# A new order for a recurrent attention and feed-forward kernel: four more units turned by DMA, and the weights loaded through ScalarE

## The chip, the core and the metric

The kernel runs on one core of a Trainium2 chip. A core has five engines that run side by side and wait for each other through semaphores: TensorE (PE in the profile; its weight loads are PEld), VectorE (DVE), ScalarE (ACT), GpSimd (POOL) and SyncE (SP), which here only issues DMAs. TensorE writes to PSUM, eight banks of 512 floats in each of 128 partitions; the other data lie in SBUF, and inputs and outputs in HBM. The metric is the time of one execution on the device in microseconds (us). Before the change it was 156.16 us, the median of three runs (154.19, 156.16 and 156.34).

## What is computed

The first half is a recurrence over 768 steps, for 4 batches and 8 heads with a state of 48 by 48 each; the second half is a feed-forward block over all 3072 tokens.

```
for t in range(S):                                  # S = 768, D = 48
    cur     = (u * k_t)[:, None] * v_t[None, :]
    y_t     = r_t @ (state + cur)
    state   = w_t[:, None] * state + k_t[:, None] * v_t[None, :]
x    = y, heads side by side                        # 3072 x 384
h    = x @ w_in                                     # 3072 x 1024
solu = h * softmax(h)
ln   = (solu - mean) / sqrt(var + 1e-6) * g_ln
out  = ln @ w_out                                   # 3072 x 384, float32
```

## The kernel before, in words

The 768 steps are cut into 6 chunks of 128, and a **unit** is one chunk of one batch: 24 units, numbered chunk first, so that unit i needs the state that unit i-4 left. Each unit passes through the same steps. Four loads of 192 KB bring w, k, r and v (`LW`, `LK`, `LR`, `LV`), head by head in rows of 192 bytes. ScalarE takes the logarithm of w (`lw`), TensorE sums it along the chunk (`cum`), ScalarE exponentiates (`ex`), and VectorE multiplies k and r by the result (`kp`). The scaled k and r are turned, so that channels lie in partitions: either by eight TensorE transposes (`krk`, `krr`) and a copy out of PSUM (`kr`), or by one transposing DMA (`kt`). TensorE makes the scores (`M`), VectorE or ScalarE copies and masks them (`m`, with GpSimd's `sel` where ScalarE copies), and TensorE makes y from the scores, v and the state (`Y`; `y` copies it out). GpSimd makes the bonus term (`p`, `q`, sometimes `qh`, `dv`; VectorE's `dg` sums it). `S`, `et` and `st` make the next state, in units 0 to 19.

For the feed-forward half y is turned too, by three TensorE transposes and a copy (`X`, `xT`) or by one transposing DMA (`xt`). `H` multiplies by w_in, `e` exponentiates on ScalarE, `he` multiplies on VectorE, `hq` squares, `Oa` and `Ob` are the two halves of the product with w_out, and `sq`, `qm`, `lv`, `rs` and `o` normalise; `out` stores. There are two forms of this half. In the first, `H` is 24 products of 128 columns that give h already turned, and `Oa` and `Ob` also make the sums of e and of the squares by products of one column (fewer where GpSimd first adds e's halves, `ea`). In the second, for units that have an `ht`, `H` is 6 products of 512 columns, ScalarE sums while it exponentiates and squares (`sv` then prepares one scalar), one transposing DMA of 256 KB (`ht`) turns the product he, and `Oa` and `Ob` have no one-column products. Weights come in by `LI` (three loads of 512 KB) and `LO` (two of 768 KB), and `wi`, `gw`, `mn`, `mc` and `ce` cast, scale and centre them.

The order is written out by hand, as one long string, `ORDER`. A word such as `kr12.d` names a step, a unit and how it is done: for a copy the engine (a, d, p for ScalarE, VectorE, GpSimd), for a load its queue (nothing for SyncE, a for ScalarE, g for GpSimd), for a TensorE step its PSUM bank. The program goes through the words, and each engine gets its instructions in just this order: a wrapper, `InOrder`, ties every instruction to the one before it on the same engine. All of them are recorded in the wrapper, so nearly every line of the profile says L84 and groups are told apart by their tiles. DMA issues stand in the order of the engine that issues them, so a load on ScalarE's queue holds ScalarE's later work until it is issued. In the built program the DMAs of SyncE's and ScalarE's queues share eight completion semaphores in turn: each issue waits until the DMA eight places before it has landed.

```
        for hp in range(HP):                      # krk and krr: four TensorE transposes each
            pe.transpose(L["kr_ps"][:, j * HP + hp, :],
                         t[:, j, 2 * hp:2 * hp + 2, :].rearrange("t a d -> t (a d)"), ident)
...
    def turned_kr(i, x):                          # kt
        sp.dma_start_transpose(out=kr_s[i % NKP], in_=kp_t[i % NKP].rearrange("t a h d -> t (a h d)"))
```

Buffers are rings: 7 for each of the inputs, 10 for lw and v in bf16, 6 for the scaled and turned k and r, 4 for most of the feed-forward half. Before the change `kt` and `xt` serve units 16 to 23, and `ht` serves units 16 to 21.

Of the kernel before, what the change touches and what calls it, by code (L numbers as in the profile page):

```python
# [18 lines left out]


ORDER = """
LW0 ih0 LW1.a LW2.a LU0 LR0 LG0 LK0.a lw0 hot13.0 cum0.0 LR1 LK1.a LR2 LK2.a ex0 LV1 LW3 LV2.g LW4 LW5 ik0 lw2 kp0
us0.4 lw1 p0 cum1.5 LR3 LK3 uc0 ex1 cum2.0 kp1 ex2 LV3.g krk0.2 p1 kp2 q0 hot3.3 krk1.6 vb1.a LV0.a krr0 lw3 LR5
LK5 kr0.d krr1 LV4.g q1 hot1.0 M0.3 vb2.a kr1.d m0.d LK4.a LR4 krk2.7 p2 q2 lw4 lw5 dg0 krr2 M1.5 cum3.2 kr2.a LW6
ex3 S1.0 LW7 m1.d LV6.g hot1.1 cum5.6 LW9.a dg1 M2.4 kp3 vb0.a p3 dv0 ex5 LK7 vb3.a cum4.1 m2.d kp5 ex4 krk3.3 q3
et1 LR7.a dv1 LW8 LR6 LK6 S0.5 krr3 Y0.i7 et0 LV8.g dg2 kr3.a y0.a kp4 S2.6 et2 p4 st0 st2 lw6 LW10 vb4.a M3.1 lw7
dg3 krk4.3 Y1.i6 LR8.a p5 krk5.7 lw9 krr4 krr5 cum7.4 dv3 m3.d y1.a X1.6 ex7 q4 LV5.g kr5.a kr4.d dv2 LR9 LK8 LK9
xT1.a vb6.a st1 S3.1 M4.2 LI1.a X0.0 q5 kp7 et3 p6 cum6.4 xT0.d gs0.7 p7 ex6 Y2.i6 dg4 m4.d S4.0 gc0 vb8.a M5.2 LV7
lw8 kp6 Y3.i7 y2.a q6 LI2 krk7.4 st3 y3.a dv4 krk6.5 vb5.a cum8.6 et4 m5.d LI0.a S5.1 st4 ex8 dg5 cum9.2 LO1 ex9
krr6 krr7 LK10 kp8 q7 kp9 kr6.a krk8.0 et5 p8 krr8 wi1.p dg6 lw10 kr7.d X2.5 vb7.p LR10.a xT2.a kr8.a S6.6 Y4.i3  # L30
dg7 X3.5 xT3.d S8.7 et6 st5 y4.a dv5 LO0 S7.5 et8 et7 wi2.a LW14 st6 M6.3 Y5.i2 st8 M7.6 cum10.0 LW13 dv7 m6.d
wi0.p y5.a m7.d LR14.a ex10 X4.2 LV9.g st7 H0.3 xT4.d krk9.5 LV10 q8 LW12 qh8 LR11 gw7.a gw5.a dv6 LV13.g H1.6 LK12
LK14 kp10 e0 gw6.a Y6.n0 he0 krk10.1 krr9 X5.2 gw4.a gw2.d e1 gw0.a krr10 gw1.a gw3.p p10 y6.d xT5.d he1 kr9.d p9
dg8 kr10.a LW15 H3.3 e3 mn0.0 mc0 LR12 ce6.d Y7.i2 hq0.a H2.5 vb9.p y7.a lw14 ce4.d he3 ce0.p ce3.d ce2.d M10.1
LW11.a ce7.p ce5.p M9.3 S9.7 m10.a et9 m9.d ce1.p LK11 st9 LR15 cum14.0 e2 lw12 hq1.a he2 LV11.g Oa0.2 M8.3 Ob0
X7.7 ex14 m8.d LV12 kp14 q9 hq3.d lw11 xT7.a Oa1.5 LW16 LR13.a cum11.3 X6.7 Ob1 xT6.d LK13 sq0 LW17 cum12.0 krk14.7
ex11 dv8 q10 kp11 lw13 sq1 Y8.n6 krr14 qm1 qm0 ex12 H4.3 lv0 y8.d kp12 vb11.p lv1 ea3.p rs1 rs0 vb10.p ea2.p LR17
p12 o0.d sel10 krk11.6 o1.a cum13.0 kr14.d out1 dg9 hq2.a ex13 krr11 Oa3.2 kr11.d e4 out0 vb12.p q12 krk12.7 kp13
Ob3 lw15 sq3 lw17 LR16.a Oa2.5 cum15.0 krr12 qm3 he4 LK17.a p11 LK15 dv9 q11 krk13.6 Ob2 ex15 S10.3 S11.4 p14 lv3
LW21 kr12.d LV16.a rs3 kp15 LK16 LK19 sq2 et10 o3.a qm2 et11 Y9.i7 krr13 lv2 cum17.0 st10 lw16 y9.a rs2 st11 ex17  # L40
o2.a out3 ea4.p S12.2 kr13.d cum16.3 dg11 et12 H5.6 kp17 p15 ex16 st12 kp16 e5 hq4.a p13 dg10 X8.5 LW19 H7.0 vb13.p
e7 he5 H6.2 out2 e6 LV18.g dg12 he7 dv10 S13.4 LK18 Oa4.7 he6 et13 krk15.6 LR20 lw19 hq5.a Ob4 q13 M12.0 xT8.a sq4
krr15 LV15.g st13 dv12 m12.a qm4 qh13 Y10.n3 Oa5.2 M11.0 M13.4 Ob5 lv4 rs4 sel12 kr15.d LV17 o4.a q14 LV14 vb14.p
X9.7 m11.a hq6.d y10.d q15 X10.3 LW18 LR19 sq5 M14.0 m13.d ea6.p lw18 LK20 dv11 xT9.d qm5 LR22.a cum19.4 lv5 xT10.d
hq7.d rs5 H8.6 m14.d sel11 dg13 dv13 o5.a ex19 e8 LK22.a kp19 H9.2 out4 ea7.p Oa6.0 cum18.4 LW20 he8 e9 Ob6 LR18
S14.6 Y11.n7 lw20 ea9.p ex18 he9 sq6 p16 qm6 kp18 out5 lv6 H10.1 rs6 o6.d hq9.a et14 dg14 st14 e10 dv14 Y12.n4
Oa7.0 y11.d LW22 y12.d vb16.a cum20.5 hq8.a ex20 q16 Ob7 ea8.p LK21 sq7 kt16 vb15.a dg15 he10 kt17 lw22 kp20 qm7
p17 Y14.n3 Oa9.7 X11.4 xT11.a lv7 q17 out6 y14.d rs7 S16.2 Y13.n1 ea10.p y13.d et16 Ob9 o7.a M15.3 sq9 kt18 st16
qm9 m15.a M17.0 LW23 M18.5 Oa8.2 m17.d M16.3 lv9 cum22.0 rs9 o9.a vb17.a LK23 out7 p19 LV21 hq10.a ex22 out9 m18.d
Ob8 m16.d qh16 dg16 LV19 dg17 kt19 H11.5 sq8 lw21 Oa10.3 X12.4 p20 e11 qm8 kp22 xT12.a lv8 X13.7 xT13.d dv15 he11  # L50
dv17 sel15 q20 Ob10 rs8 sq10 q19 o8.a qm10 lv10 rs10 out8 X14.4 H12.0 Y17.n7 Y15.n2 xT14.d e12 dv16 hq11.a H13.5
e13 o10.d ea11.p y15.d he12 y17.d LR23 p18 out10 LV22 he13 vb18.p ea12.p hq12.a H14.3 Y16.n7 LR21 Oa11.0 q18
cum21.1 Ob11 e14 qh19 y16.d ex21 vb19.d he14 sq11 p22 hq13.a S15.6 qm11 kt22 lv11 rs11 dg18 dv18 o11.a Oa12.7 et15
X15.5 Ob12 ea13.p kt20 sq12 kp21 M19.3 xT15.d p23 qm12 xt16 lv12 st15 Y18.n2 H15.0 rs12 out11 ea14.p LV23 o12.a
dg20 m19.d lw23 e15 y18.d ea15.p dg19 he15 H16.6 dv19 out12 Y19.n5 cum23.2 Oa13.4 vb23.p hq14.a xt17 kt21 S17.0
ex23 kp23 q23 Ob13 p21 q22 LV20 xt18 vb21.a e16 sq13 Oa14.1 qm13 H17.2 kt23 lv13 y19.d et17 rs13 o13.a he16 sv16
vb20.p M21.4 hq15.a e17 M20.6 st17 out13 Ob14 sq14 dg23 m20.d Oa15.0 dv23 qm14 vb22.p m21.a S19.7 Ob15 xt19 he17
ht16 q21 lv14 rs14 o14.a sel21 sq15 qm15 lv15 et19 M23.3 m23.d out14 dv20 M22.1 ht17 rs15 H18.5 qh21 m22.a dg21
o15.a out15 e18 dv21 Y20.n4 y20.d dg22 xt20 hq16.a Y21.n2 S18.1 et18 y21.d dv22 hq17.a sel22 he18 H19.3 xt21 st18
Oa16.0 Oa17.2 e19 st19 ht18 hq18.a Y22.n1 Ob16 sq16 y22.d Ob17 he19 qm16 lv16 xt22 sq17 H21.5 sv18 Y23.n7 qm17  # L60
Oa18.4 sv17 rs16 lv17 rs17 e21 o16.d ht19 hq19.a o17.d H20.0 y23.d out16 e20 Ob18 sq18 out17 he21 xt23 H22.5 qm18
lv18 e22 hq21.a rs18 Oa19.7 ht21 H23.2 ea22.p sv19 o18.a Ob19 he20 he22 hq22.d sq19 qm19 Oa21.0 Oa22.4 e23 ht20
lv19 rs19 hq20.a Ob21 he23 sq21 ea23.p o19.a out18 Ob22 hq23.d qm21 out19 sv21 sq22 qm22 lv22 rs22 Oa20.3 o22.d
lv21 out22 rs21 o21.d Oa23.6 Ob20 sq20 qm20 sv20 lv20 Ob23 sq23 rs20 qm23 out21 lv23 rs23 o23.a o20.d out20 out23
"""

NIO, NLW, NKP, NWK, NHT = 7, 10, 6, 4, 4
# [559 lines left out]
```

## Time and profile before

| | |
|---|---|
| median of three runs | 156.16 us (154.19 to 156.34) |
| the profiled execution, its own time | 151.6 us |
| its span in the profile | 149.7 us |
| mean granted TensorE clock | 0.966 |
| busy: TensorE, VectorE, ScalarE, GpSimd | 130.6, 122.3, 122.1, 116.0 us |
| DMA | 31.50 MB, mean 210 GB/s |
| SyncE's queue (q1), ScalarE's (q10), GpSimd's (q0) | 74.1%, 14.3%, 4.4% of 16 engines |
| loads issued by SyncE, ScalarE, GpSimd | 71, 21, 11 |
| transposing DMAs, all by SyncE | 8 of k and r, 8 of y, 6 of he |

Busy is the time in which an engine has an instruction under way; TensorE's are pipelined, so that it can be busy and still not at its peak. The DMA share is the mean over the core's 16 DMA engines; as packets overlap it can pass 1. The profiled execution was 4.6 us shorter than the median of the timed runs.

### The profile page before, as it was taken

The numbers are of one execution on the slowest core, as the hardware profiler recorded it, in microseconds if no ns is written. First come the engines' busy times: TensorE is split into PE (matmuls) and PEld (weight loads), VectorE is DVE, ScalarE is ACT, GpSimd is POOL, SyncE is SP. The second block draws the span as 40 slices with busy tenths as digits, with TensorE's granted clock in tenths as the row PEclk, the third lists the DMA queues.
The fourth block names the chain that finished last, engine by engine and source line by source line (L and its number), as shares of the span: only waits on it lengthen the run. The fifth ranks groups of instructions, "written<-read, shape, count | busy, mean of one in ns | idle before, by whom it ended". The sixth has DMA issues, their size and how long they took to land. (4 is left out here: it accounts for less than half of the span.)

```text
span 149.7 us, 4668 instructions
## 1 busy us (share of the span) xinstructions
PE 130.6 (87%) x1804; PEld 95.3 (64%) x1809; DVE 122.3 (82%) x211; ACT 122.1 (82%) x266; POOL 116.0 (77%) x147
## 2 busy tenths in 40 slices
PE   6957439787599989999999999999999999899970
PEld 2325227565389856878977887689886566558540
DVE  5059759799588999999999989998997988776750
ACT  3297667696669988998998889998989999798951
POOL 7599587996799397999999999989999998103300
PEclk9999975899959999999999999999999999999999
DMA  5999999999999899989998999895978687479342
GB/s 104 255 287 262 278 239 210 246 286 316 362 322 254 174 204 226 204 215 246 244 239 180 224 220 217 174 203 146 198 184 185 119 194 210 100 173 166 88 158 105
DMA packets 112199, 31.50 MB, mean 210 GB/s; under 512 B 107161, under 2 KB 111266, under 8 KB 112178
## 3 DMA queue, kind: packets, MB, share of 16 engines
q1 hardware_dynamic: 91426, 24.26, 74.1%
q10 hardware_dynamic: 20048, 4.79, 14.3%
q0 software_dynamic: 704, 2.16, 4.4%
q8 instruction: 14, 0.23, 0.6%
q14 instruction: 7, 0.06, 0.1%
HBM read 22.03 MB, written 4.72 MB: 179 GB/s over the span
## 5 line engine op out<-in xcount | busy, mean ns | idle before, releaser
L84 PE MATMUL ps<-w,he 128*128 128x385 bf16 x192 | 42.4, 325 | 0.7 <-DVE st L84 0.4
L84 DVE TENSOR_TENSOR kp<-ps,kr_in 128x768 bf16<-128x768 f32 x24 | 22.9, 952 | 11.0 <-ACT ps L84 6.9
L84 POOL TENSOR_TENSOR p<-kr_in 128x384 bf16<-128x384 f32 x24 | 23.9, 1003 | 4.6 <-DMA kr_in<-in_k_dram 3.6
L84 PE MATMUL ps<-xT,win_sb 128*128 128x128 bf16 x432 | 27.0, 220 | 0.0
L84 POOL TENSOR_TENSOR ea<-e 128x512 bf16<-128x512 bf16 x15 | 17.7, 1184 | 11.0 <-ACT e L84 11.0
L84 PEld LDWEIGHTS <-win_sb 128*128 128x128 bf16 x432 | 25.2, 99 | 0.7
L84 ACT ACTIVATE e<-ps 128x1024 bf16<-128x1024 f32 x24 | 24.4, 1020 | 0.9 <-PE ps L84 0.8
L84 ACT ACTIVATE ps<-ps 128x768 f32<-128x768 f32 x24 | 19.1, 802 | 6.1 <-PE ps L84 6.0
L84 PE MATMUL ps<-one_col,hq 128*128 128x1 bf16 x144 | 23.6, 164 | 0.0
L84 DVE TENSOR_TENSOR he<-ps,e 128x1024 bf16<-128x1024 f32 x18 | 21.7, 1216 | 1.5 <-ACT e L84 1.4
L84 POOL TENSOR_TENSOR q<-p,u_bc 128x384 bf16<-128x384 bf16 x24 | 22.5, 939 | 0.2
L84 PEld LDWEIGHTS <-he 128*128 128x128 bf16 x192 | 18.0, 96 | 7.1 <-DMA he<-win_f 1.3
L84 DVE TENSOR_TENSOR m<-ps,keep 128x1024 bf16<-128x1024 f32 x18 | 21.7, 1216 | 0.4 <-PE ps L84 0.4
L84 POOL TENSOR_TENSOR dv<-vb,dg 128x384 bf16<-128x384 bf16 x24 | 19.9, 832 | 1.9 <-DVE dg L84 1.2
L84 PEld LDWEIGHTS <-kp 128*128 128x128 bf16 x208 | 13.9, 101 | 6.2 <-DVE kp L84 2.2
L84 ACT ACTIVATE lw<-w_in 128x384 bf16<-128x384 f32 x24 | 12.4, 525 | 4.2 <-DMA w_in<-in_w_dram 4.2
L84 PEld LDWEIGHTS <-kr 64*128 64x128 bf16 (+1 forms) x272 | 11.0, 97 | 6.2 <-issue 2.7
L84 PEld LDWEIGHTS <-hq 128*128 128x128 bf16 x144 | 11.2, 96 | 5.6
L84 ACT ACTIVATE hq<-he 128x1024 bf16<-128x1024 bf16 x13 | 13.7, 1053 | 0.0
L84 PE MATMUL ps<-ident,kp 128*128 128x128 bf16 x128 | 11.6, 231 | 1.6 <-DVE kp L84 1.6
L84 DVE TENSOR_REDUCE dg<-q 128x8 f32<-128x384 bf16 (+1 forms) x24 | 11.9, 500 | 0.4 <-POOL q L84 0.4
L84 PE MATMUL ps<-lw,uti_neg 128*128 128x384 bf16 x24 | 8.2, 344 | 3.2 <-DVE m L84 1.2
(97 smaller groups left out, 294.2 us busy)
## 6 DMA issues: line engine op xcount, KB each, us to landing
out_dram<-o SPq DMA_DIRECT2D x24, 192.0 KB, 2.3
w_in<-in_w_dram SPq DMA_DIRECT2D x20, 192.0 KB, 4.9
kr_in<-in_k_dram SPq DMA_DIRECT2D x18, 192.0 KB, 4.9
kr_in<-in_r_dram SPq DMA_DIRECT2D x17, 192.0 KB, 5.2
v_in<-in_v_dram POOLq DMA_DIRECT2D x11, 192.0 KB, 4.5
v_in<-in_v_dram SPq DMA_DIRECT2D x11, 192.0 KB, 4.3
wout_f<-in_moe_w_out_dram SPq DMA_DIRECT2D x2, 768.0 KB, 7.1
kr_in<-in_r_dram ACTq DMA_DIRECT2D x7, 192.0 KB, 5.1
```

Of the source, the lines that this page charges most:

```text
L84: made = make(*args, **kwargs)
```

## The change

Only the string `ORDER` changes; no function does. All its 43 lines are new, since the words stand in another sequence and most PSUM banks differ. What the words do is nearly the same, with these differences:

- Units 12 to 15 are turned by DMA. Their `krk`, `krr`, `kr`, `X` and `xT` go, and `kt`, `xt`, `ht` and `sv` come: `kt` and `xt` now serve units 12 to 23, `ht` units 12 to 21. With `ht` these four units take the second form of the feed-forward half.
- Queues: SyncE issues 63 loads instead of 71, ScalarE 33 instead of 21, GpSimd 7 instead of 11. All five loads of w_in and w_out are ScalarE's, and stand farther apart: they were between the 39th and the 42nd load of the order, and are between the 30th and the 49th.
- `ea` goes for units 2, 3 and 12 to 15, and comes for unit 5; `qh` serves nine units instead of five; `sel` five instead of six.
- Engines: VectorE has 2 `kr`, 2 `xT`, 1 `hq` and 1 `gw` fewer, 1 `m` and 1 `o` more; ScalarE has 2 `kr`, 2 `xT`, 1 `m`, 1 `o`, 5 `vb` and 1 `wi` fewer and 1 more `hq`; GpSimd has 5 more `vb`, 1 more `gw`, 1 more `wi`.
- Unit 2 leads the start instead of unit 0, and 16 products on zeros (`hot`) keep TensorE going instead of 18.

```
-LW0 ih0 LW1.a LW2.a LU0 LR0 LG0 LK0.a lw0 hot13.0 cum0.0 LR1 LK1.a LR2 LK2.a ex0 LV1 LW3 LV2.g LW4 LW5 ik0 lw2 kp0
+LW1.a LW0.a LW2 LR1.a lw2 hot10.0 cum2.0 lw1 LW5.a ex2 LV4.g LK2 LV6.g LR2 cum1.2 lw0 LK1 LW4.a ex1 hot2.4 cum0.4
...
-LW21 kr12.d LV16.a rs3 kp15 LK16 LK19 sq2 et10 o3.a qm2 et11 Y9.i7 krr13 lv2 cum17.0 st10 lw16 y9.a rs2 st11 ex17
+S10.1 dv8 S8.0 p11 LR16 H5.6 Y8.n2 ce2.d hq1.a et10 LV11 y7.a st13 M10.3 LK15 st10 m10.d kt12 LW19 p12 lw14 et8
...
-dv17 sel15 q20 Ob10 rs8 sq10 q19 o8.a qm10 lv10 rs10 out8 X14.4 H12.0 Y17.n7 Y15.n2 xT14.d e12 dv16 hq11.a H13.5
+p21 rs8 o8.d xt14 H12.4 dg17 lv11 rs11 p19 S17.1 dg16 ex23 out8 kp23 q19 e12 o11.a et17 dv16 dv17 H15.6 he12 M18.2
+Oa10.0 hq13.a Y16.n4 m18.d Ob10 p22 kt20 y16.d e15 sq10 p20 out11 st17 hq12.a q20 qm10 ht12 lv10 LV22.a qh20 he15
...
-lv18 e22 hq21.a rs18 Oa19.7 ht21 H23.2 ea22.p sv19 o18.a Ob19 he20 he22 hq22.d sq19 qm19 Oa21.0 Oa22.4 e23 ht20
-lv19 rs19 hq20.a Ob21 he23 sq21 ea23.p o19.a out18 Ob22 hq23.d qm21 out19 sv21 sq22 qm22 lv22 rs22 Oa20.3 o22.d
+e22 ea22.p o18.d o19.d out18 hq20.a sv20 Oa20.2 out19 he22 H23.3 sv21 out17 e23 Ob20 sq20 hq22.d ea23.p qm20 lv20
+rs20 he23 o20.a hq21.a Oa21.5 Oa22.0 Ob21 hq23.d Ob22 sq21 qm21 sq22 lv21 qm22 lv22 rs21 rs22 out20 o22.d o21.a
```

## The prediction, written before the changed kernel ran

> **What bounds the kernel now.** I read the page's busy times and its 40 slices first.
>
> ```profile
> span 149.7 us, 4668 instructions
> PE 130.6 (87%) x1804; PEld 95.3 (64%) x1809; DVE 122.3 (82%) x211; ACT 122.1 (82%) x266; POOL 116.0 (77%) x147
> ...
> PE   6957439787599989999999999999999999899970
> PEclk9999975899959999999999999999999999999999
> DMA  5999999999999899989998999895978687479342
> ```
>
> Every engine is busy for over three quarters of the span, so the sums settle little. In the slices (3.74 us each) TensorE has holes up to the eleventh slice, about 41 us, and hardly any from there to 140 us. DMA is full from the second slice on and thins out late. Next come the stretches, with each engine's busy time, and behind it the granted clock, the DMA share and GB/s.
>
> ```profile
> 0.00:62.00 62.00, 48.62 (x613) 33.82 (x615) 48.26 (x89) 45.09 (x85) 50.35 (x74) 0.92 1.08 252
> 62.00:86.00 24.00, 24.00 (x388) 19.72 (x386) 23.62 (x39) 22.16 (x47) 23.22 (x27) 1.00 0.99 220
> 86.00:120.00 34.00, 33.89 (x547) 26.10 (x546) 31.05 (x53) 32.00 (x68) 33.11 (x38) 1.00 0.88 183
> 120.00:141.00 21.00, 20.41 (x233) 13.50 (x233) 16.42 (x26) 19.11 (x51) 9.29 (x11) 1.00 0.77 151
> ```
>
> Up to 62 us the DMA share is over 1: the loads set the pace. From 62 to 120 us TensorE has no hole at all. What TensorE waited for from 40 to 136 us, in us, times and longest, bears that out:
>
> ```profile
> PE ps L84 <- DVE he L84: 0.6, 1, 0.6
> PE ps L84 <- DVE st L84: 0.4, 1, 0.4
> ```
>
> As a busy TensorE need not be at its peak, I took the spacing of its steps from its timeline (start, duration, what), where one starts right behind the other:
>
> ```profile
> 61.50 1.50 PE L84 MATMUL ps<-xT,win_sb 128*128 128x128 bf16 x24
> 62.83 0.39 PE L84 MATMUL ps<-ident,kp 128*128 128x128 bf16 x4
> 63.06 0.33 PE L84 MATMUL ps<-lw,uti_neg 128*128 128x384 bf16 x1
> ...
> 131.88 0.82 PE L84 MATMUL ps<-w,he 128*128 128x385 bf16 x4
> 132.54 1.46 PE L84 MATMUL ps<-win_sb,xT 128*128 128x512 bf16 x6
> 133.83 0.82 PE L84 MATMUL ps<-w,he 128*128 128x385 bf16 x4
> ```
>
> The reader sees H in its first form at 62.83 - 61.50 = 1.33 us, four transposes at 0.23, half an output in the second form at 0.66 and H in the second form at 1.29. Half an output in the first form took 0.81 (63.60 to 64.41, with `ea`) or 0.86 without. Adding such spacings over the order, 95.7 us of TensorE work stand at and behind the first H, which started at 43.55 us. That ends at 139.3 if nothing is late; TensorE really ended at 144.9. So **TensorE bounds the kernel from 43 us on** with 5.6 us lost, ahead of it the loads do, and the last 5 us are the chain of the last unit's normalisation and store.
>
> **The change, part by part.**
>
> *Units 12 to 15 on TensorE.* Their 64 step-wise transposes of k and r go: 8 groups of four, 1.8 us. `X` took 0.17 a unit: 0.7 us. H becomes 0.04 shorter a unit: 0.2 us. Eight halves of output go from 0.81 to 0.66: 1.2 us. `ea` gone for units 2 and 3 and new for 5 costs 0.1 net. Sum: **3.8 us less** in the stretch that TensorE bounds. The two `hot` products fewer lie ahead of it and count nothing; as they bridge a hole that the loads make, they would cost nothing either way.
>
> *The other engines.* VectorE: 2 `kr` (0.68), 2 `xT` (0.35), one `hq` (0.71), one `gw` (1.09) less, one `m` (1.22) and one `o` (0.61) more, four sums halved (0.20 each): 2.9 us less. ScalarE: 2 `kr` and one `m` (1.01), 2 `xT` (0.48), 5 `vb` (0.51), one `o` (0.58), one `wi` (1.04) less; one `hq` (1.05), eight read-outs of sums (0.20) and four `sv` (0.19) more: 4.8 us less. GpSimd: 5 `ea` (1.18), 4 load issues (0.94), one `sel` (1.14) less; 5 `vb` (0.52), 4 `qh` (0.55), one `gw` (1.27), one `wi` (1.04) more: 3.7 us less. None of them pays by itself, but each has to follow a TensorE that is 3.8 us quicker over 100 us. VectorE was busy for 23.62 of 24 us at 62 to 86, so there it has only its own saving to give.
>
> *Twelve more transposing DMAs.* SyncE issues all of them. Rows of SyncE's issues, with the shortest, median and longest duration in ns:
>
> ```profile
> L84 SPq DMA_TRANSPOSE kr<-kp x8: 1243/1262/2879, 86.5 to 118.1; - x8
> ...
> L84 SPq DMA_TRANSPOSE xT<-y x8: 1190/1210/2239, 109.3 to 133.6; - x8
> ...
> L84 SPq DMA_TRANSPOSE he<-win_f x6: 1240/1250/1278, 121.4 to 136.6; - x6
> ```
>
> Four of each: 4 x (1.26 + 1.21 + 1.25) = 14.9 us more on SyncE's queue, less 8 load issues at about 0.45 = 3.6 us. The landing comes 3.2, 2.4 and 3.1 us after the issue. Data: 4 x (256 + 96 + 256) KB = 2.49 MB. From 120 to 141 us, where only transposes and stores run, 21 us at 151 GB/s are 3.17 MB in 0.77 x 21 = 16.2 us of DMA time, 5.1 us a MB; so 12.7 us of DMA time are added, all of it where loads still come. Room up to the 1.08 of the start: 24 x 0.09 + 34 x 0.20 = 9.0 us. This is close. Bounds: nothing, if transposes and loads overlap (from 106 to 108 us the trace has both at once at a share of 1.45), and 12.7 - 9.0 = 3.7 us late. I take nothing, since from the middle of the kernel on most loads lay ready long before use: for v of unit 18 the landing was at 77.6 and its use at 105.9.
> [...]
>
> *ScalarE's 33 load issues instead of 21.* An issue waits for the landing of the DMA eight places earlier, and holds ScalarE. The timelines of ScalarE and TensorE show what that costs when it goes wrong:
>
> ```profile
> 38.20 0.41 ACTq L84 DMA_DIRECT2D kr_in<-in_r_dram  x1
> 38.65 0.48 ACT L84 COPY xT<-ps 128x384 bf16<-128x384 bf16 x1 [2.34 <-DMA v_in<-in_v_dram]
> ```
>
> ```profile
> 39.18 0.33 PE L84 MATMUL ps<-ident,y 128*128 128x128 bf16 x3 [1.99 <-ACT xT L84]
> ```
>
> ScalarE stood 2.34 us before a load of r could be issued, the copy of `xT` behind it was late, and TensorE stood 1.99 us for that copy. Two of 21 issues did so (the other 1.26 us); most hide behind the running instruction. At that rate 12 more cost ScalarE 2.1 us; bounds 0 and 12 x 2.34. I take no net change, since ScalarE saves 4.8 us.
> [...]
>
> *The start and the spread weights.* Up to 62 us at 252 GB/s 15.6 MB came: 3.15 MB of weights, in some 9.5 us at the 316 to 362 GB/s of the slices they came in, and 63 loads, (62 - 9.5) / 63 = 0.83 us each. The second H stands behind 50 loads and all weights, with 94.1 us of TensorE work at and behind it: 41.5 + 9.5 + 94.1 = 145.1. In the new order the worst such place is the third H, behind 57 loads, with 86.2: 47.3 + 9.5 + 86.2 = 143.0, so 2.1 us less and not 3.8. Where the loads hold the start, 1.7 us of the gain go. Bounds 0 and 1.7; I take 0.9.
>
> *The end.* The last `ht20` landed 5.2 us after its issue instead of 3.1, and the output behind it started only then. The new order puts `Oa20` ahead of the last H, with more outputs behind: bounds 0 and -2.1, taken -0.4.
>
> Sum: -3.8 + 0.9 - 0.4 = **-3.3 us**. On the profiled execution's own 151.6 us (149.7 span and 1.9 around it) that is 148.3, or -2.2%. The median stood 3.0% above that execution; 148.3 x 156.16 / 151.6 = **152.8 us**. A measurement of this kernel tells about 2% from no change: 153.0 and 159.3 are the borders.
>
> **The rivals.** (1) *The gain is not followed.* VectorE, ScalarE or one of ScalarE's late issues holds TensorE, which gives its 3.8 us back as new holes. For it: 23.62 of 24 us on VectorE. Against: 31.05 of 34 later on. Time: 0 to -1.5 us, middle 155.4; chance 0.22. (2) *The transposes take over, and the kernel is slower.* The place is SyncE's queue and the DMAs behind it between 62 and 120 us. For it: room 9.0 against 12.7 us, and at 106 to 138 us SyncE already issued nearly back to back. Decided at 9.0 us of DMA time for the twelve, 0.75 us each; beyond that loads and turned tiles are late and TensorE waits, its gain gone: +3.7 us, 155.3 x 1.030 = 160.0. Against: landing was long ahead of use. Chance 0.28. (3) *The saving is not there*, as the transposes moved were hidden: excluded by a TensorE without holes while they ran, so I fold it into (1).
>
> **How the numbers follow.** The forecast has 0.50, spread from 149.0 (start free, `ht20` on time, first scaled k about 1 us earlier: -6.9 us) to 154; 0.41 of it is under 153.0. Rival 1 adds 0.02 to faster and 0.20 to same; rival 2 has 0.24 beyond 159.3 and 0.04 below. Faster 0.43, same 0.33, slower 0.24. The range goes from 149.0 to 160.5.
>
> **What would show it.** TensorE's records 162 fewer; no hole over 0.6 us between 45 and 135 us; its end near 141.5. A DMA share above 0.95 from 62 to 120 us without new waits on landings would clear the transposes. Wrong would be: TensorE waiting for `kr`, `xT` or `he` landings, or ScalarE idle ahead of load issues for more than 5 us in all.

## The result

| | before | after |
|---|---|---|
| median of the timed runs, same chip | 155.18 us | 168.12 us (166.37 to 169.23, 4 runs) |
| ratio to before, 95% interval | | 1.094 (1.069 to 1.119): slower |
| the profiled execution: its own time, its span | 151.6, 149.7 us | 166.37, 164.5 us |
| TensorE's last product ends | 144.9 us | 159.6 us |

The forecast was 152.8 us, the range 149.0 to 160.5; the kernel came out beyond the range, even beyond the slower rival's 160.0. The ratios here and below use only runs within 1.5% of the fastest of the same kernel, so they are not the quotients of the medians. First the page of the kernel after: its header, then TensorE's busy time, the granted clock and the DMA share in 40 slices of 4.11 us.

```profile
span 164.5 us, 4367 instructions
PE 134.2 (82%) x1640; PEld 94.2 (57%) x1647; DVE 123.0 (75%) x207; ACT 115.9 (70%) x267; POOL 111.8 (68%) x148
...
PE   6726747895647999999999979299999899799970
PEclk9985765579995589999999999959999999999996
DMA  5999999999999999946899999996799577775613
```

TensorE has 164 records fewer (162 were forecast, and the two programs have 1808 and 1646 products), and yet is busy 3.6 us longer. Its row is no longer full from the twelfth slice on: there is a hole near 103 us and several late ones. The clock row, all but full in the kernel before, has fives and sixes in the first 60 us and a five at 107 us. The same stretches as in the prediction (each engine's busy time, then granted clock, DMA share, GB/s):

```profile
0.00:62.00 62.00, 43.79 (x467) 30.68 (x469) 39.10 (x74) 34.47 (x66) 45.31 (x69) 0.75 1.11 251
62.00:86.00 24.00, 23.62 (x381) 18.53 (x380) 23.66 (x39) 22.64 (x49) 20.27 (x26) 1.00 0.86 176
86.00:120.00 34.00, 29.54 (x405) 22.26 (x406) 26.91 (x44) 24.78 (x57) 25.79 (x30) 0.95 1.05 212
120.00:141.00 21.00, 20.23 (x238) 12.32 (x238) 20.12 (x32) 17.48 (x50) 16.24 (x22) 1.00 0.82 171
```

Up to 62 us TensorE did 467 products where it had done 613, at a mean clock of 0.75 instead of 0.92, and from 86 to 120 us it stood 4.5 of 34 us. What TensorE waited for from 40 to 136 us, and the longest of ScalarE's waits over the whole run (us, times, longest):

```profile
PE ps L84 <- DVE he L84: 3.5, 2, 3.2
PE ps L84 <- ACT m L84: 2.2, 2, 1.2
PE ps L84 <- DVE kp L84: 1.9, 3, 0.9
```

```profile
ACT ps L84 <- DMA kr_in<-in_k_dram: 5.5, 2, 4.4
...
ACT lw L84 <- POOL q L84: 4.0, 1, 4.0
ACT e L84 <- DMA w_in<-in_w_dram: 3.5, 1, 3.5
...
ACT vb L84 <- DMA kr_in<-in_r_dram: 2.2, 1, 2.2
```

TensorE hardly waited for a landing; it waited for what VectorE and ScalarE make. But ScalarE's own list is full of landings of tiles that the named instruction does not read: `ps` is no reader of k, `vb` none of r. In each case a load issue stands between the two and was the one that waited. ScalarE's waits that end with a landing sum to 20.7 us after, 7.8 us before; without those of the logarithm `lw` for w, which it does read, to 18.8 and 3.6 us.

To place the loss I took two sums from the traces, behind 43 us, where TensorE sets the pace: TensorE's idle time, and half of its busy time in the stretches at half clock (the clock's records are 1.0 or 0.5 and nothing else).

| kernel | TensorE's end | idle behind 43 us | at half clock behind 43 us | work in it | so lost |
|---|---|---|---|---|---|
| before | 144.9 | 1.8 | 1.2 | 1.2 | 0.6 |
| after | 159.6 | 10.8 | 13.6 | 12.5 | 6.2 |

Idle 9.0 us more and half clock 5.6 us more make 14.6 of the 14.7 us by which TensorE ended later. That is a little too good: at 45 us the work still to come, added at the prediction's spacings, ended at 136.0 against 139.1 us, so the kernel after was 3.1 us ahead then, and about 3 us more were lost in ways that these two sums don't show. (These projected ends are estimates: with the mean spacings of the two traces instead, the lead at 45 us comes out as 1.4 us.) At 65 us the same sum ended at 148.2 against 142.3, at 110 us at 155.9 against 144.3: the loss came in steps, at 45 to 65 and at 95 to 110 us.

### The profile page after: what moved, and what is told of

Its sections match the earlier page's. It is cut to its first block, busy times and chain, and to the rows that moved or that the text cites. A ratio compares the mean times of both kernels' runs of the same rounds, so it can differ in the third digit from the quotient of the medians.

```text
span 164.5 us, 4367 instructions
## 1 busy us (share of the span) xinstructions
PE 134.2 (82%) x1640; PEld 94.2 (57%) x1647; DVE 123.0 (75%) x207; ACT 115.9 (70%) x267; POOL 111.8 (68%) x148
## 4 chain that ended last, share of the span: by engine, by line
PE 28%; DMA 24%; POOL 15%; ACT 12%; issue 9%; DVE 5%; SPq 4%; ACTq 2%; DVEq 0%; POOLq 0%
PE ps L84 28%; DMA w_in<-in_w_dram 8%; DMA kr_in<-in_k_dram 5%; POOL q L84 5%; POOL p L84 4%; DMA kr_in<-in_r_dram 3%; SPq L84 3%; ACT e L84 3%; DMA win_f<-in_moe_w_in_dram 3%; DMA he<-win_f 3%; ACT hq L84 2%; DMA xT<-y 2%; ACT o L84 2%; POOL vb L84 2%; ACTq L84 2%
## 5 line engine op out<-in xcount | busy, mean ns | idle before, releaser
L84 DVE TENSOR_TENSOR kp<-ps,kr_in 128x768 bf16<-128x768 f32 x24 | 22.7, 952 | 14.7 <-ACT ps L84 14.7
L84 PE MATMUL ps<-xT,win_sb 128*128 128x128 bf16 x336 | 24.0, 237 | 0.4 <-DVE kp L84 0.2
L84 PEld LDWEIGHTS <-win_sb 128*128 128x128 bf16 x336 | 22.5, 108 | 1.9 <-issue 0.6
L84 DVE TENSOR_TENSOR m<-ps,keep 128x1024 bf16<-128x1024 f32 x19 | 23.1, 1216 | 0.3 <-PE ps L84 0.2
L84 DVE TENSOR_TENSOR he<-ps,e 128x1024 bf16<-128x1024 f32 x14 | 17.0, 1217 | 6.9 <-ACT e L84 6.9
L84 POOL TENSOR_TENSOR ea<-e 128x512 bf16<-128x512 bf16 x10 | 11.5, 1154 | 14.9 <-ACT e L84 13.8
L84 PE MATMUL ps<-one_col,hq 128*128 128x1 bf16 x112 | 18.4, 164 | 0.4 <-DVE hq L84 0.4
L84 PE MATMUL ps<-kr 64*128 64x128 bf16 x192 | 10.5, 237 | 5.7 <-DVE kr L84 3.0
L84 PE MATMUL ps<-win_sb,xT 128*128 128x512 bf16 x54 | 14.1, 379 | 0.3
L84 DVE TENSOR_TENSOR st<-ps,et 128x384 bf16<-128x384 f32 x20 | 10.6, 548 | 3.5 <-ACT et L84 3.5
L84 DVE TENSOR_TENSOR win_f<-ps,e 128x1024 bf16<-128x1024 f32 x10 | 12.2, 1216 | 0.5 <-ACT e L84 0.4
```

The costliest lines, as they stand in the source:

```text
L84: made = make(*args, **kwargs)
```

## The experiments

The times are medians; the ratio is to the kernel before, timed on the same chip at the same time.

| edit | us | ratio (95%) |
|---|---|---|
| the order of after, the queues of before | 165.83 | 1.081 (1.066 to 1.096) |
| the order of before, the queues of after | 168.99 (163.81 to 170.26) | none on record; before: 153.73 |
| start of before, rest of after | 166.16 | 1.104 (1.096 to 1.112) |
| start of after, rest of before | 168.10 | 1.115 (1.105 to 1.125) |
| after, units 12 to 15 turned by TensorE | 168.01 | 1.102 (1.087 to 1.117) |
| after, 29 load issues from ScalarE to SyncE | 172.81 | 1.148 (1.136 to 1.160) |
| before, three load issues from SyncE to ScalarE | 170.05 | 1.129 (1.121 to 1.138) |
| after, three load issues off ScalarE | 162.05 | 1.058 (1.049 to 1.068) |
| after, five load issues off ScalarE | 161.15 | 1.063 (1.054 to 1.072) |
| after, 33 idle products in TensorE's holes | 164.48 | 1.077 (1.069 to 1.084) |
| before, 17 idle products in TensorE's holes | 154.66 | 1.011 (0.994 to 1.028) |
| before, units 12 to 15 turned by transfers | 171.78 | 1.129 (1.118 to 1.139) |
| the same, transfers placed by the trace | 164.51 | 1.077 (1.068 to 1.086) |
| the same, eleven stores by GpSimd | 164.16 | 1.080 (1.067 to 1.092) |
| after, eleven stores by GpSimd | 169.44 | 1.117 (1.108 to 1.126) |
| after, all three remedies | 163.08 | 1.073 (1.062 to 1.083) |
| before, twelve transposing transfers more | 167.41 | 1.091 (1.077 to 1.105) |
| before, twelve plain copies more | 162.79 | 1.060 (1.042 to 1.077) |

### Which part of the change: queues, order or turned units

Two kernels exchange the queue letters of the loads (51 words each), one turns units 12 to 15 back, one puts nearly all load issues on SyncE, and two join the halves of the orders at about 60 us.

```
 e1: LW1.a LW0.a LW2 LR1.a ...   ->  LW1.a LW0 LW2.a LR1 ...      (order of after)
 e4: kt12 ... xt12 ... ht12 sv12 ->  krk12.7 krr12 kr12.d ... X12 xT12 ...  (units 12 to 15)
 e6: LW4.a LK5.a LR5.a ...       ->  LW4 LK5 LR5 ...              (29 words)
 s1: words of before up to its second H, then what is left, in the order of after
```

The order of after with the queues of before:

> The changed kernel, with every load on the queue that it has in the kernel before; the order of the words stays. Theory A (ScalarE stands at its load issues until the DMA eight places back has landed; waits of ScalarE that end with a landing grew from 7.8 to 20.7 us): ScalarE's waits on landings fall to 8 to 11 us and the span from 164.5 to 150 to 156. Theory B (the twelve new transposing DMAs fill the DMA): no change, 162 to 166. Theory C (the sequence itself is poor, whatever the queues): 160 to 166, with the holes of TensorE up to 60 us still there.

The order of before with the queues of after:

> The kernel before, with every load on the queue that the changed kernel gives it. Theory A: ScalarE's waits on landings rise from 7.8 to 15 us or more and the span from 149.7 to 156 to 162. Theory B and theory C: within 2 us of 149.7.

After, units 12 to 15 turned by TensorE:

> The changed kernel, with units 12 to 15 turned by TensorE again and their feed-forward half in the first form (without the added halves of e); queues and the rest of the order stay. Theory A and theory C: it stays slow, 162 to 170. Theory B: the span falls to 150 to 156.

After, without ScalarE's issues:

> After, with all load issues of ScalarE behind the first few moved to SyncE's queue at the same places of the order, so that ScalarE never stands at a load issue that waits for an earlier landing (20.7 us in after, 7.8 us in before). If ScalarE's standing is the cause: the difference of 12.9 us comes back, 155 to 158 us. If not: some 20 more issues on SyncE (about 0.45 us each, 9 us) and the same waits now standing in SyncE's queue, ahead of the transposing transfers: 165 to 172 us, with TensorE waiting for landings instead of for ScalarE.

The two joined orders:

> The order of before up to its second H (about the first 60 us), and the order of after for everything that is then left. By the projected end (time plus TensorE work still to come) after had lost 5.6 us on before by 60 us and another 12.5 us behind that. Theory 'start' (the loads of the first 60 us come late, and the rest of after only carries that on, because its loads and turned tiles then meet at 82 to 98 us): with before's start the later loss goes too, 150 to 156 us. Theory 'rest' (the order behind is itself what loses): 12.5 us of it stay, 162 to 166 us. Theory 'fit' (each half is fitted to the other's times, so any mixture loses at the seam): over 165 us.

> The mirror: the order of after up to its H of unit 1 (about the first 62 us), then the order of before for what is left, so that units 12 to 15 are turned by TensorE. Theory 'start': the late loads of the start do it, 162 to 168 us, and the curve of the projected end goes on rising behind 62 us as in after. Theory 'rest': only the 5.6 us of the start are lost, 157 to 160 us, with a flat projected end behind 65 us. Theory 'fit': over 165 us with new holes right behind the seam.

Measured: medians between 165.8 and 172.8 us. Turning the four units back changed nothing (168.01 against 168.12), so in the kernel after the turned units, taken whole, are not what costs: they seem to give back just the 3.8 us that they should save. Giving the queues back brought 1%, which lies inside the intervals; giving the order back ranged from 163.81 to 170.26 us and brought nothing clear of noise. Yet with the queues of before ScalarE's waits that end with a landing fell from 20.7 us to this one:

```profile
ACT lw L83 <- DMA w_in<-in_w_dram: 4.0, 1, 4.0
```

That meets the condition of theory A, but not its time of 150 to 156 us, so ScalarE's held issues alone are not the loss. In that profile TensorE waited for turned tiles instead, 5.0 us behind 43 us where it had been 1.1. The joined orders were as slow as after in both directions; of the three theories written down only "fit" allows both, the first of them by 1 us. The kernel with all but four of ScalarE's issues taken away was the slowest of the six: SyncE then had those issues and their waits ahead of the transposing transfers, and TensorE's waits for turned k and r rose to 5.6 us. What follows is that no part of the change, taken out by itself, gives the loss back: every mixture was some 8 to 15% slower than the kernel before. That the order of before is fitted to its own queues is a reading of this, not shown by it. So I went to single instructions.

### Three load issues on ScalarE

The kernel before, with three words changed (of the five weight transfers two were ScalarE's already, so three move; the expectation's twelve is wrong):

```
-... LI2 ... LO1 ... LO0 ...
+... LI2.a ... LO1.a ... LO0.a ...
```

> Before, with only the twelve transfers of the two weight matrices issued by ScalarE as in after, all else untouched. With all of after's queues in the order of before it was 169.0 us, its delay coming in one jump of 11 us at 34 to 41 us. If the weights on ScalarE make that jump (each of their issues waits for the landing eight places back and holds the casts and read-outs behind it): 162 to 169 us, with 15 to 20 us of ScalarE's waits ending with a landing. If the other moved queues (k, r, v, gates) make it: 154 to 158 us.

Measured: 170.05 us, 17 us for three letters. The timelines of ScalarE and TensorE in that kernel (start, duration, what; in brackets the idle time before it and what ended it) show how:

```profile
46.73 0.48 ACT L84 CAST y<-ps 128x384 bf16<-128x384 f32 x1
54.92 0.37 ACTq L84 DMA_DIRECT2D kr_in<-in_r_dram  x1
55.42 0.80 ACT L84 ACTIVATE ps<-ps 128x768 f32<-128x768 f32 x1 [8.21 <-POOL vb L84]
```

```profile
57.25 0.48 PE L84 MATMUL ps<-st,kr 128*128 128x96 bf16 x4 [6.41 <-DVE kp L84]
```

ScalarE reached the load of r of unit 14 at 47.2 us and could issue it at 54.92; `ex` of unit 10 stood behind it for 8.2 us, and TensorE 6.4 us for that, of the 18.4 us by which it ended later. In the kernel before the same load was issued at 42.24 without a wait. Nobody had touched it. The built program tells why. The transfers of SyncE and ScalarE share eight completion counters in turn, and an issue waits until the counter's previous transfer has landed: in the trace of after, 26 of ScalarE's 33 issues have that landing on record, none went ahead of it, and 16 went 0.02 to 0.08 us behind it. The turns go by the order of the instructions in the built program, which is not that of the list: with more loads on ScalarE, its issues come farther back there. In the kernel before, r of unit 14 takes its turn behind three SyncE loads that stand later in the list, and follows k of unit 10, which had landed at 42.11 us; with three letters changed it takes it behind thirteen such loads and follows k of unit 11, which landed at 54.8 us. Summed over ScalarE's issues that have a transfer eight turns ahead, such overtaking transfers of SyncE are 32 in before (21 issues in all), 78 here, and 204 in after (33 issues).

In the kernel after this is the chain of waits from 40 to 66 us (start, duration, what):

```profile
39.91 5.69 DMA kr_in<-in_r_dram
45.60 0.02 issue
45.62 4.62 DMA win_f<-in_moe_w_in_dram
...
53.28 5.85 DMA w_in<-in_w_dram
59.13 0.02 issue
59.15 0.37 ACTq L84
...
59.62 0.04 ACT e L84
```

The third part of the first weight matrix could only be issued 0.02 us after r of unit 12 had landed, whose counter it takes; and at 59.15 us v of unit 14 could only be issued when w of unit 17 had landed. Behind that issue stood the first exponential `e` of the hidden layer, for 3.5 us, for a v that is used at 75 us. So I took these issues away:

```
-... LI2.a ... LO1.a ... LV14.a ...
+... LI2 ... LO1 ... LV14.g ...
```

> After with three load issues taken from ScalarE's queue: the third part of the first weight matrix and the second half of the other one to SyncE, v of unit 14 to GpSimd. In after ScalarE stood 2.2, 2.5 and 3.5 us at these three before the casts, copies and read-outs behind them, and the chain of waits from 40 to 66 us runs through the first and the third. Issue theory: of these 8.2 us about 5 come back in the first output of the hidden layer (it starts at 59.6 us in after), and with it some of the half clock, 161 to 164 us. If the first 60 us are bound by the loads themselves or the later part loses on its own: 166 to 169 us.

Measured: 162.05 us, ratio 1.058 against 1.094. Three of 921 words are worth 6.1 us of the medians. TensorE ended at 155.1 us, 4.5 us earlier: idle 10.0 us, half clock 6.8 us. At 85 us the projected end was 143.7 us, level with the kernel before; the rest was lost behind that. The chain there led to the next such issue, in the kernel after at 99 to 103 us:

```profile
102.12 0.89 POOL q L84
103.01 0.36 ACTq L84
...
104.16 0.70 ACT e L84
104.86 0.02 issue
104.89 1.24 DVE he L84
```

That is v of unit 23, used at 136 us. The chain names GpSimd's `q`, which ended at the same time, but the issue needs nothing of it. It needs the buffer, free since GpSimd had cast v of unit 16:

```profile
95.03 0.50 POOL L84 CAST vb<-v_in 128x384 bf16<-128x384 f32 x1 [1.00 <-DMA v_in<-in_v_dram]
```

And it needs its completion counter, whose transfer eight turns earlier is r of unit 22: that landed at 102.92 us, and the issue went at 102.99. So the counter held this issue too, and not the buffer, as the next expectation has it. ScalarE stood 4.0 us there with the exponential of unit 11 behind, and TensorE had its hole of 3.2 us. Two words more:

```
-... LR21.a ... LV23.a ...
+... LR21 ... LV23.g ...
```

> The kernel with three issues moved (162.05 us), and two more taken from ScalarE: v of unit 23 to GpSimd, whose own cast frees that buffer (in after ScalarE stood 4.0 us at this issue, at 99 to 103 us, for a load that is used at 136 us, and the exponential of unit 11 stood behind it; in the kernel with three issues moved 3.4 us), and r of unit 21 to SyncE (1.2 us). Issue theory: TensorE's hole of 2.2 us at 99.5 us goes and with it the half clock at 103.0 to 106.4 us that takes 1.7 us, 158 to 159.5 us. If the loads of 82 to 98 us are late in any case (v of units 16 and 19 land 0.1 to 0.8 us ahead of their use): 161 to 163 us, with a hole of the same length elsewhere.

Measured: 161.15 us, ratio 1.063 (1.054 to 1.072), so no change against 1.058. The wait and the hole of 2.2 us went, as the theory of issues has it, and TensorE's idle time behind 43 us fell from 10.0 to 8.6 us; but it ended only 0.5 us earlier. Holes of 1.2 and 0.6 us at 90 to 93 us (for turned k and for scaled k) are in the kernel with three issues moved as well, 1.9 us earlier, so this execution was already behind there, and the half clock came at 93.6 to 97.0 us instead of 103.0 to 106.4. The time is that of the second expectation; its reason, that the loads of 82 to 98 us are late in any case, is not shown by it, as no new hole of the same length opened.

### The half clock

The kernel after in windows of 4 us from 44 us (TensorE's busy time first, then weight loads, VectorE, ScalarE, GpSimd; granted clock, DMA share, GB/s), and TensorE's timeline:

```profile
44.00:48.00 4.00, 2.52 (x52) 2.12 (x50) 1.44 (x3) 1.98 (x6) 3.60 (x4) 1.00 1.07 220
48.00:52.00 4.00, 2.76 (x31) 1.93 (x32) 3.53 (x5) 1.51 (x3) 1.71 (x2) 0.62 1.07 267
52.00:56.00 4.00, 3.28 (x23) 1.94 (x23) 2.53 (x3) 4.00 (x7) 3.53 (x5) 0.50 0.97 262
56.00:60.00 4.00, 4.00 (x47) 4.00 (x45) 2.30 (x4) 0.50 (x2) 2.86 (x4) 0.60 1.04 205
```

```profile
54.87 4.92 PE L84 MATMUL ps<-xT,win_sb 128*128 128x128 bf16 x48
```

Two H in the first form took 4.92 us; the next two, at 60.5 us and full clock, 2.94. TensorE had been loosely filled from 40 to 52 us, and the clock was half from 49.0 to 59.2 us, just when the dense work began. To see whether that costs anything I filled the holes with products on zeros:

```
-... S7.6 ... S9.3 ... M9.0 ... cum12.6 ... Y13.n4 ... cum19.2 ...
+... hot3.3 S7.6 ... hot4.4 S9.3 ... hot4.6 M9.0 ... hot5.5 cum12.6 ... hot3.5 Y13.n4 ... hot14.1 cum19.2 ...
```

> After with 33 idle products more on TensorE (the kernel's own warm-up words, no result uses them), put where its trace has holes: three ahead of the sum of unit 7, four ahead of that of unit 9, four and five in the holes at 48 and 52 us, three and fourteen in those at 94 and 103 us. At full clock one takes 0.22 us, so they are as long as the holes. Clock theory (after TensorE's looser stretches the granted clock is half, at 49.0 to 59.2 and 107.0 to 110.4 us, and the 12.5 us of work in those 13.6 us take 6.2 us longer than at full clock): the half clock at 49 and 107 us goes, 4 to 6 us come back, 162 to 164 us. If the clock follows the lost time and doesn't cause any (the loads end last anyway): 168 us as before, or 1 to 3 us longer by products that stand in the way.

```profile
44.00:48.00 4.00, 3.72 (x58) 2.76 (x57) 1.04 (x2) 1.49 (x4) 3.38 (x4) 1.00 0.99 194
48.00:52.00 4.00, 3.71 (x43) 2.05 (x42) 3.97 (x6) 1.57 (x4) 1.25 (x2) 1.00 1.00 263
52.00:56.00 4.00, 2.83 (x44) 2.06 (x43) 2.13 (x3) 3.88 (x7) 3.99 (x5) 1.00 1.00 261
```

Measured: 164.48 us (163.95 to 165.02, after had 166.37 to 169.23). The clock stayed full behind 43 us, and TensorE ended 2.4 us earlier. So the half clock costs, but 2.4 us by TensorE's end or 3.6 by the medians, and not the 6.2 of the table: at 60.0 us a new hole of 1.9 us opened, as TensorE, now quicker, came to the same late exponential. In the kernel before, whose half clock lies mostly where the loads set the pace:

> Before with 17 such products more in its own holes at 20.5, 34.5 and 37.2 us (eight, four, five). Its clock is half at 20.3 to 27.1 and 40.8 to 44.2 us. Clock theory: the work at 40.8 to 44.2 us, where TensorE begins to set the pace, goes 1 to 2 us faster, ratio 0.985 to 0.995. If the loads end last there: no change, ratio 1.00; if a product holds a step whose load has landed: up to 1.02.

Measured: 1.011 (0.994 to 1.028), nothing. Its half clock behind 20 us fell from 10.2 to 3.4 us, without a gain.

### What the transfers cost by themselves

The kernel before with units 12 to 15 turned by transfers, first with each transfer at the place of the TensorE step that it replaces, then each where SyncE comes after its input is ready by the trace of before:

```
-... krk12.7 ... krr12 ... kr12.d ... X12.4 ... xT12.a ... ea12.p ...      (and 13, 14, 15)
+... kt12 ... xt12 ... sv12 ... ht12 ...
```

> The kernel before, with units 12 to 15 turned by transposing DMAs and their feed-forward half in the second form; queues and the rest of the order stay. Theory A and theory C: the transposes do no harm, the 3.8 us of TensorE's work come through in part, span 146 to 150. Theory B: the DMA fills up between 62 and 120 us, TensorE gets holes there, span 155 to 163.

> Before with units 12 to 15 turned by transposing transfers as in the earlier run that took 171.8 us, but each transfer put in SyncE's queue where SyncE came after its input was ready in the trace of before, so that SyncE need not stand for an input. If the 20 us lost there were SyncE standing (first of all for k of unit 14): 153 to 158 us, as the prediction had it for the turned units alone. If the transfers' own 1.25 us on SyncE's queue and their DMA time are what delays the loads behind them (in before the loads of k and r of units 15 to 19 and w of units 18 to 20 land 0.0 to 2.5 us ahead of their use): 160 us and more, with TensorE waiting for loads from 68 us on.

Measured: 171.78 and 164.51 us, 1.129 and 1.077. So 5% was SyncE standing for inputs with loads queued behind it, and 8% remain. TensorE saved its 3.8 us at first (projected end 135.4 at 45 us); by 85 us that was used up, and from 100 to 150 us another 15 us went, with 9.2 us of waits for turned tiles behind 43 us. SyncE's queue stood back to back from 111 to 152 us there, from 111 to 153 us in after. To free it I gave eleven stores to GpSimd, in both kernels:

```
-... out7 ... out17 ...
+... out7.g ... out17.g ...
```

> After, with the eleven stores of units 7 to 17 issued by GpSimd instead of SyncE. In after SyncE issues back to back from 111 to 153 us, its transposing transfers at 1.2 to 1.3 us each and these stores at 0.3 to 0.5 us. Theory that SyncE's queue bounds the end: the eleven stores are 4.7 us of that queue, 3 to 5 us come back, 163 to 165 us, and the turned tiles are issued that much earlier. Theory that the transfers' own time or TensorE bounds it: 167 to 169 us.

> The kernel before with units 12 to 15 turned by well placed transfers (164.5 us), and its eleven stores of units 7 to 17 issued by GpSimd. SyncE stood back to back from 111 to 152 us there. Theory that SyncE's queue is the price of the turned units: 4 to 5 us come back, 159.5 to 161 us, with the waits of TensorE for turned tiles (9.2 us behind 43 us) halved. If the transfers themselves are slow: 163.5 to 165.5 us.

Measured: 169.44 and 164.16 us, no gain in either. This did not tell the theories apart: GpSimd now stood for the tiles to be stored, 13.7 us in the kernel after, ahead of its own casts and masks. Three remedies at once, the stores, the three issues and 24 idle products:

> After with all that the runs pointed to: the three load issues off ScalarE, 24 idle products in the holes of that kernel's trace (four, eight, three, nine), the eleven stores on GpSimd. If the three causes add up: 162.05 less 3.4 us of half clock less 4 us of SyncE's queue, 154 to 157 us, level with before. If each covers another (the next wait is as late as the one taken away): 160 to 163 us.

Measured: 163.08 us, no better than the three issues alone. They do not add up, as if each wait covered another. (In that kernel the half clock came earlier, at 37.0 to 47.3 us, products or not.)

The last two kernels measure the price directly. Twelve transfers more in the kernel before, with no work taken away, once transposing and once plain:

```
-... kt16 ... xt16 ... ht16 ...          (and 17, 18, 19)
+... kt16 xd16.kt ... xt16 xd16.xt ... ht16 xd16.ht ...
+    def extra(i, x):   # same source, into memory that nothing reads; x[1] == "c": plain
+        sp.dma_start_transpose(out=to.rearrange("p (a b) -> p a b", b=128), in_=src)
```

> The kernel before with twelve transposing transfers more, on SyncE's queue: each right behind that of k and r, of y and of he of units 16 to 19, with the same source, into memory that nothing reads. No work goes from any engine. The prediction's price for twelve: 0, at most 3.7 us, as DMA time; 152 to 156 us. Theory that SyncE's queue is the price: at 106 to 138 us it issues back to back, eight of the twelve stand there at 1.25 us, 8 to 10 us less what can slide, 158 to 163 us, with TensorE waiting for turned tiles.

> The same twelve places, sources and bytes (2.49 MB), but plain copies, whose issue takes about 0.45 us on SyncE instead of 1.25. Theory SyncE's queue: 12 times 0.45 us, 3.6 us of them where it issues back to back, a third of what the other kernel loses, 155 to 157 us. Theory DMA time: about as much loss as the other kernel, as the bytes are the same. If neither costs anything: 152 to 154 us.

Measured: 1.091 (1.077 to 1.105) and 1.060 (1.042 to 1.077), 12.9 and 8.3 us of the medians. SyncE's timeline with the transposing ones and with the plain ones, then TensorE's waits from 86 to 155 us, in the same sequence:

```profile
132.15 1.26 SPq L84 DMA_TRANSPOSE he<-win_f  x1
133.46 1.30 SPq L84 DMA_TRANSPOSE wout_f<-win_f  x1
```

```profile
128.14 1.19 SPq L84 DMA_TRANSPOSE xT<-y  x1
129.38 0.58 SPq L84 DMA_DIRECT2D win_f<-y  x1
```

```profile
PE ps L84 <- DMA kr<-kp: 6.1, 4, 2.5
PE ps L84 <- DMA xT<-y: 4.7, 3, 1.9
PE ps L84 <- DMA he<-win_f: 2.5, 2, 1.3
```

```profile
PE ps L84 <- DMA kr<-kp: 2.9, 3, 2.5
PE ps L84 <- DMA he<-win_f: 2.6, 1, 2.6
```

Transfers that nobody needs made TensorE wait 13.3 us for the tiles issued behind them, where it had waited for none, and plain ones 5.5 us. The bytes are the same, so it is not the bytes alone; the two waits stand as 2.4 to 1, the lengths of one issue on SyncE's queue, 1.3 and 0.58 us, as 2.2 to 1. That speaks for the time on the queue as what makes the tiles late.

The whole loss does not follow it so closely. TensorE ended 15.1 and 11.5 us later. The two sums of the table above place it: idle time behind 43 us rose by 13.5 and 7.3 us, and the half clock cost 1.7 and 5.1 us, where it had been 0.6. With the plain transfers the clock was half for 10.2 us behind 43 us (3.4 with the transposing ones), which would explain why they cost two thirds and not less than half; no run takes the half clock out of that kernel. All issues of SyncE together took 120.4 us before, 136.5 and 131.5 us here, but that sum is no fixed price: with idle products alone and the same transfers it was 113.8 us. ScalarE's waits for landings did not rise (4.4 and 6.5 us against 7.8). Whether DMA time has a part stays open: the share rose from 0.87 to 1.09 and 1.11 at 86 to 106 us, and from 0.68 to 0.74 and 0.80 at 120 to 138. The twelve also take turns of the completion counters and hold their source tiles longer, which no run separates.

No kernel that ran was faster than the one before.

## Why the prediction was wrong

**What bounds the kernel** was right for the kernel before and was its undoing. TensorE has no hole from 43 us on, and many of the loads and copies ahead of it come just in time. I read that as "the others have room"; the runs say that a delay ahead of it can pass on to TensorE and is not made up again (15.1 us at TensorE's end for twelve transfers that nobody needs).

**TensorE's own 3.8 us.** The work did go: 162 products fewer in the program, 164 records in the trace, and at 45 us the projected end stood 3.1 us ahead by the estimate above. Not priced was the clock. All spacings came from rows at full clock, and the 96 us of work were taken as a constant; after ran 12.5 us of it at half clock. I had the clock row before me, and in the kernel before it hardly mattered behind 43 us (0.6 us). Size: 2.4 to 3.6 us by the run with idle products, which also fill holes.

**The other engines' savings**, counted as nothing, brought nothing.

**Twelve more transposes, taken as 0, bound 3.7 us.** This step failed, in the choice of the price. I had worked out 14.9 us on SyncE's queue and then weighed 12.7 us of DMA time against 9.0 us of room instead. Twelve transfers alone cost the kernel before 12.9 us, three and a half times the bound; some of that came by way of the half clock. The reason given for 0, that loads lay ready long before use, rested on v of unit 18, one of the loosest. In the same trace k of units 15 to 17 landed 0.7, 2.2 and 0.1 us ahead of their use, r of unit 18 0.5, w of units 18 and 20 0.0. A full table of these slacks would have forbidden the 0. In the kernel after the price shows only as the 3.8 us that the turned units do not bring (turning them back: no change); that other waits cover the rest there is argued, not shown.

**ScalarE's twelve more issues, taken as no net change** ("at that rate 2.1 us", bounds 0 and 28). This step failed too. The mechanism was named rightly, an issue waits for the transfer eight turns earlier and holds ScalarE; the size was wrong, because I took a rate per issue from a kernel in which two of 21 had gone wrong. ScalarE's waits for landings that its instructions don't read went from 3.6 to 18.8 us, within the bounds and seven times the addition of 2.1. Three issues make 6.1 us of the result. The turns were in the built program and could have been read before the run: 204 overtaking transfers against 32. It was also no help that ScalarE saves 4.8 us of work: what stands behind a held issue is late by the wait, however idle the engine is later (`ex` of unit 10 by 8.2 us, with three letters changed).

**The start, taken as a loss of 0.9 us.** Until 45 us nothing was lost. The first H started at 54.9 us instead of 43.55 all the same. It stands 37 products farther back in the new order, and at the end it did not wait for weights (the third part was cast at 51.3 us): TensorE reached it late through holes of 0.9 to 1.4 us, and at half clock from 49.0 us on. With the three issues moved it started at 52.1 us.

**The end** was never reached on time, so its 0.4 us can't be judged.

**The rivals.** The slower one had the right sign and, by the twelve transfers in the kernel before, the right place, "SyncE's queue and the DMAs behind", but a wrong measure: it was to be decided at 9.0 us of DMA time and to cost 3.7 us. The first rival named "one of ScalarE's late issues", and let it give back at most the gain. Neither had a loss beyond the gain worked out; as TensorE had no slack anywhere, that loss had no bound from the saving.

**What would show it.** ScalarE idle ahead of load issues for more than 5 us was named as a sign of being wrong, and came true. The other sign, TensorE waiting for turned tiles, came true with 1.1 us in after. The test that would clear the transposes was not met: the DMA share was 0.86 at 62 to 86 us, below the 0.95 that it asks for. It told little either way, as turning the units back changed nothing.

The move of loads to ScalarE's queue won no bandwidth: up to 62 us the DMA share was 1.08 before and 1.11 after, the rate 252 and 251 GB/s. Nor was the time of an issue small beside the transfer. In the two kernels with twelve transfers more, a plain copy of 256 KB took 0.58 us of issue and 2.5 to 2.8 us to its landing, a transposing one 1.3 and 3.0 to 3.8 us; and in the kernel before SyncE's issues, one behind the other, fill 120.4 of 149.7 us.

**What stays open.** With five issues moved the kernel is still 6% slower than before, with the queues of before 8%. The traces name a next wait each time, and taking it away brought the next; I can't say which property of the order is behind them; that it was not fitted to when the loads land on this chip is my guess, not shown.

## What to carry to other kernels

Before a step is moved onto a queue, list for every load and turned tile how long it lies ready before its use; where the list has zeros, each issue put ahead of them is paid at least in part, by its time on that queue: here twelve transposing transfers, at 1.3 us of issue, made TensorE wait 13.3 us for the tiles behind them, twelve plain ones, at 0.58 us, 5.5 us. An engine that computes and also issues loads holds all its computing behind an issue that may not go yet (ScalarE stood 8.2 us behind one load of r), so give it only loads whose buffer and completion counter are free when it gets there, and read the counters' turns from the built program. And price work on TensorE by the clock that it will get: a loosely filled stretch ahead of dense work cost the kernel after 2.4 to 3.6 us more.

## What the runs showed of the hardware

- TensorE's clock halved without a long hole. From 36 to 49 us of the kernel after no hole was longer than 1.5 us, but only 1.88 and 2.52 of 4 us were filled at 40 to 48 us, and the clock was half from 49.0 to 59.2 us. Half-clock stretches were 3.4, 6.8, 10.2 and 13.7 us long in the clock records of before and after, but for those that the end of the record cuts.
- A transposing transfer of 256 KB took 1.3 us of SyncE's queue and landed 3.8 us (from the scaled k and r) or 3.0 us (from he) after its issue, a plain copy of the same bytes 0.58 and 2.8 or 2.5 us (medians of four each in the two kernels with twelve more).
- A completion counter can hold an issue that its buffer does not: v of unit 23 stood until r of unit 22 had landed at 102.92 us, 7 us after its own buffer was free.
- One trace is one execution: freeing SyncE of stores, in the kernel before with turned units, ended TensorE 2.8 us earlier in the profiled execution (156.4 against 159.2 us) and changed nothing in the medians; the first was the shortest of its four runs, the second the longest.
